# The order of the tensors in SBUF, in a decode attention kernel that streams K and V

## The chip, the cores and the metric

The kernel runs on one core of a Trainium2 chip. The metric is the device time of one execution in microseconds (us); before the change it is 2565.35 us, the median of three runs (2564.96 to 2565.8).

## The reference

Two independent attention blocks, A and B, for one new token each. Per block there are 8 batch rows, 32 heads of 128, and a cache of 4096 keys and values per head, all in bf16:

```python
q = (x @ wq).reshape(B, Sq, H, Dh).transpose(0, 2, 1, 3)
scores = einsum("bhqd,bhkd->bhqk", q, k_cache) * (Dh ** -0.5)
o = einsum("bhqk,bhkd->bhqd", softmax(scores, axis=-1), v_cache)
return o.transpose(0, 2, 1, 3).reshape(B, Sq, H * Dh) @ wo
```

The outputs of A and B stand side by side in a result of 8 x 1 x 2048. K and V of both blocks are 1.07 GB, each byte of which is read once; the weights `wq` and `wo` are 8.4 MB each.

## The kernel before

The work is cut into 64 turns (32 per block). A turn takes one batch row and eight heads: 8 x 4096 keys of 128 values are 8.39 MB, laid out as 128 partitions with 256 keys each, so each partition gets one contiguous row of 65,536 bytes. A load of K or V is one DMA of 128 such rows. `kbuf` holds two K loads (128 x 2 x 32768 bf16), `vbuf` one V load (128 x 32768 bf16); together they are 196,608 bytes of each partition. `wq` goes through `vbuf`, `wo` through the first half of `kbuf`, and the last V through `kbuf`.

In turn n, VectorE multiplies K in place with the query, which is the same in all rows of a head (line 337, four pieces of 64 keys). TensorE adds up 16 groups of 8 products with an identity matrix (line 347), VectorE adds the 8 that are left (line 359) and prepares the softmax (lines 364 to 368). ScalarE takes the exponentials of one head after the other (line 375). TensorE multiplies the probabilities of the turn before with V (`pv`, line 396), ScalarE copies the product (line 403), TensorE gathers the heads' diagonal blocks (line 411), VectorE scales them (line 423).

SP issues all big loads, in the order K of turn n, then V of turn n - 1 (lines 505 and 509, issued by line 223). The wait of V's load is for `pv` of the turn before, which has to be done with `vbuf`; the K load that follows in SP's order finds its half of `kbuf` already free. At the end `wo` of block B comes in five pieces (`pieces`, 16, 8, 4, 2 and 2 of 32 rows of 2048 bytes per partition) right behind the last V, and TensorE projects each piece as it lands (line 461).

Waits are worked out from the order of the operations (`Program.finish`) and the names of the tensors that they read and write; addresses play no part in them. The tensors get their addresses in the order in which the `sb` calls stand (lines 177 to 201): each begins where the one before it ends, rounded up to 32 bytes.

Of the kernel before, what the change touches and what calls it, by code (L numbers as in the profile page):

```python
# [8 lines left out]
BF16 = mybir.dt.bfloat16  # L9
FP32 = mybir.dt.float32  # L10
# [133 lines left out]
def _build(nc, caches, out):  # L144
    x0, k0, v0, wq0, wo0 = caches[0]
    B, Sq, D = x0.shape
    _, H, Sk, Dh = k0.shape
    NC = len(caches)
    HP = 8
    SEG = 128 // HP  # L150
    T = Sk // SEG
# [6 lines left out]
    TB = 512 // Dh  # L158
# [9 lines left out]
    with es:  # L168
        block = es.enter_context(nc.Block())

        def sb(name, shape, dt):
            return es.enter_context(nc.sbuf_tensor(name, shape, dt))
# [1 line left out]
        def ps(name, shape):  # L174
            return es.enter_context(nc.psum_tensor(name, shape, FP32))

        kbuf = sb("kbuf", [128, 2, T * Dh], BF16)
        vbuf = sb("vbuf", [128, T * Dh], BF16)
        prob = sb("prob", [128, T, HP], BF16)
        osb = sb("osb", [128, TB * Dh], FP32)  # L180
        asb = sb("asb", [128, CW], FP32)
        osum = sb("osum", [128, CW], FP32)
        orow = sb("orow", [128, CW], BF16)
        qT = sb("qT", [128, NC, H * B], BF16)
        qbc = sb("qbc", [128, 2, Dh], BF16)
        ident = sb("ident", [128, 128], BF16)
        ona = sb("ona", [128, NC * NG, HP, B], BF16)
        pick = sb("pick", [H, 128 + 3], BF16)
        turned = sb("turned", [H, B, Dh], BF16)
        onp = sb("onp", [128, RW, B], BF16)  # L190
        sel = sb("sel", [128, TB, HP], FP32)
        tmax = sb("tmax", [128, 32], FP32)
        rsum = sb("rsum", [128, 2, HP], FP32)
        rl = sb("rl", [128, 2, HP], FP32)
# [440 lines left out]
def bass_concat_heads__mha_block_cached__mha_block_cached__decode_kernel(  # L635
    nc, A_x, A_k_cache, A_v_cache, A_wq, A_wo, B_x, B_k_cache, B_v_cache, B_wq, B_wo, out,
):
    caches = [(A_x, A_k_cache, A_v_cache, A_wq, A_wo), (B_x, B_k_cache, B_v_cache, B_wq, B_wo)]
    _build(nc, caches, out)
# [28 lines left out]
```

## Time and profile before

| | |
|---|---|
| median of the runs | 2565.35 us |
| profiled execution, first to last instruction (span) | 2563.2 us |
| busy, TensorE matmuls / VectorE / ScalarE / GpSimd | 1470.8 / 1360.0 / 652.1 / 291.1 us |
| share of the 16 DMA engines, SP's queue | 99.9% |
| moved by DMA | 1107.52 MB in 19755 packets, 432 GB/s |

The page of the profile gives no time for the profiled execution beyond its span, so the 2.15 us between the span and the median of the runs stand for what lies around the first and the last instruction. Busy times are sums over the span; an engine that waits for a load shows the wait as idle time in front of its next instruction. A DMA packet here is one contiguous row of one partition (64 KB for K and V) or a write of a few bytes that reports completion. The packets of a stretch of the DMA view are those that start in it.

### The profile page before, as it was taken

What the parts mean: (1) busy time and instruction counts of PE and PEld (TensorE: products, weight loads), DVE (VectorE), ACT (ScalarE), POOL (GpSimd) and SP (SyncE); (2) the same over time, 40 slices, a digit from 0 to 9 for tenths busy, and PEclk for the clock granted to TensorE, in tenths of its full rate; (3) what the DMA queues carried; (4) which work ended last, traced back from release to release, by engine and by line L of the source; (5) the groups of instructions that cost most, each with busy time, mean ns of one, the idle gap of its engine ahead of it and who ended that gap; (6) DMA issues with size and microseconds to landing.
All of it is one profiled execution on the core that took longest, in us unless ns stands there. A gap on an engine that the chain in (4) does not pass through costs nothing.

```text
span 2563.2 us, 19013 instructions
## 1 busy us (share of the span) xinstructions
PE 1470.8 (57%) x9440; PEld 291.3 (11%) x5600; DVE 1360.0 (53%) x913; ACT 652.1 (25%) x1127; POOL 291.1 (11%) x112
## 2 busy tenths in 40 slices
PE   3565565565565565565565565555655655655656
PEld 0101101101101101101011011011011011011012
DVE  3456455455465465465464564564564564554551
ACT  0322322312312313313313313213223223223122
POOL 0111011011011011011011011011011010110110
PEclk8787787787787887887887887877877877878878
DMA  9999999999999999999999999999999999999999
GB/s 425 428 438 430 438 430 437 430 437 431 436 432 436 432 436 432 435 433 435 432 436 432 436 432 436 431 437 431 437 431 437 430 438 430 438 430 438 430 437 386
DMA packets 19755, 1107.52 MB, mean 432 GB/s; under 512 B 2256, under 2 KB 2320, under 8 KB 2592
## 3 DMA queue, kind: packets, MB, share of 16 engines
q1 hardware_dynamic: 19616, 1107.31, 99.9%
q8 instruction: 7, 0.11, 0.0%
q10 hardware_dynamic: 128, 0.06, 0.0%
q14 instruction: 4, 0.03, 0.0%
HBM read 1107.33 MB, written 0.03 MB: 432 GB/s over the span
## 4 chain that ended last, share of the span: by engine, by line
DMA 63%; PE 17%; DVE 14%; issue 6%; SPq 0%; another core or an unknown queue 0%; DVEq 0%
DMA kbuf<-in_B_k_cache_dram 31%; DMA kbuf<-in_A_k_cache_dram 30%; PE red L347 12%; DVE kbuf L337 12%; PE oacc L396 4%; DMA kbuf<-in_B_wo_dram 2%; DVE osb L359 2%; SPq L223 0%; DVE on L423 0%; PE acc L461 0%; DVEq L601 0%; PE oacc L275 0%; PE late L275 0%; PE bps L286 0%
## 5 line engine op out<-in xcount | busy, mean ns | idle before, releaser
L337 DVE TENSOR_TENSOR kbuf<-kbuf,qbc 128x8192 bf16<-128x8192 bf16 x256 | 1128.2, 4408 | 782.9 <-DMA kbuf<-in_A_k_cache_dram 389.8
L347 PE MATMUL red<-kbuf,ident 128*128 128x512 bf16 x4096 | 1050.9, 419 | 392.9 <-DVE kbuf L337 218.7
L375 ACT ACTIVATE prob<-osb,bias 128x256 bf16<-128x256 f32 x512 | 598.7, 1583 | 930.4 <-PE oacc L396 895.6
L425 POOL COPY ona<-on 128x8 bf16<-128x8 bf16 x64 | 278.7, 4354 | 2218.2 <-DVE on L423 2218.2
L411 PE MATMUL sps<-sel,osb 128*128 128x8 f32 x512 | 116.6, 357 | 649.9 <-ACT osb L403 649.7
L359 DVE TENSOR_REDUCE osb<-red 128x64 f32<-128x512 f32 x256 | 176.0, 687 | 305.9 <-PE red L347 305.9
L375 ACT ACTIVATION_READ_ACCUMULATOR prob<-osb,bias 128x1 f32 x512 | 252.9, 494 | 0.0
L329 ACT ACTIVATE qbc<-bps 128x256 bf16<-128x256 f32 x32 | 12.3, 383 | 897.6 <-PE bps L325 897.6
L396 PE MATMUL oacc<-vbuf,prob 128*32 128x512 bf16 x4032 | 231.8, 383 | 10.5 <-DMA vbuf<-in_B_v_cache_dram 10.5
L411 PEld LDWEIGHTS sps<-sel,osb 128*128 128x128 f32 x512 | 112.4, 323 | 669.7 <-issue 667.8
L347 PEld LDWEIGHTS red<-kbuf,ident 128*128 128x128 bf16 x256 | 25.1, 98 | 1191.0 <-issue 1170.3
L396 PEld LDWEIGHTS oacc<-vbuf,prob 128*32 128x32 bf16 x4032 | 102.5, 97 | 324.6 <-issue 219.1
L403 ACT ACTIVATE osb<-oacc 128x512 f32<-128x512 f32 x64 | 38.2, 597 | 15.3 <-PE oacc L396 8.2
L381 PE MATMUL sps<-rsum,ones 128*128 128x8 f32 x128 | 36.6, 360 | 5.4 <-ACT prob L375 5.4
L381 PEld LDWEIGHTS sps<-rsum,ones 128*128 128x128 f32 x128 | 34.7, 331 | 5.5 <-ACT prob L375 5.5
L364 DVE TENSOR_REDUCE rmax<-osb 128x1 f32<-128x256 f32 x64 | 26.9, 420 | 7.6
L423 DVE TENSOR_TENSOR on<-sps,rl 128x8 bf16<-128x8 f32 x64 | 10.1, 158 | 27.9 <-PE sps L381 27.9
L365 DVE STREAM_TRANSPOSE tmax<-rmax 128x32 f32<-128x32 f32 x64 | 13.5, 212 | 7.7
L366 DVE TENSOR_REDUCE nmax<-tmax 128x2 f32<-128x32 f32 x64 | 11.9, 186 | 7.6
L318 POOL COPY qg<-qT 128x256 bf16<-128x256 bf16 x32 | 12.5, 392 | 28.0 <-DVE qT L290 27.4
L368 DVE SCALAR_TENSOR_TENSOR bias<-nmax,neg 128x8 f32<-128x8 f32 x64 | 10.7, 168 | 7.7
L275 PE MATMUL oacc<-vbuf,orow 128*8 128x512 bf16 x64 | 7.7, 472 | 11.4 <-DMA vbuf<-in_A_wq_dram 11.4
(52 smaller groups left out, 104.1 us busy)
## 6 DMA issues: line engine op xcount, KB each, us to landing
kbuf<-in_B_wo_dram SPq DMA_DIRECT2D x1, 4096.0 KB, 39.5
kbuf<-in_B_wo_dram SPq DMA_DIRECT2D x1, 2048.0 KB, 44.0
kbuf<-in_B_wo_dram SPq DMA_DIRECT2D x1, 1024.0 KB, 46.1
kbuf<-in_B_wo_dram SPq DMA_DIRECT2D x2, 512.0 KB, 47.2
kbuf<-in_A_k_cache_dram SPq DMA_DIRECT2D x32, 49.1
vbuf<-in_A_v_cache_dram SPq DMA_DIRECT2D x32, 30.2
kbuf<-in_B_k_cache_dram SPq DMA_DIRECT2D x32, 49.1
vbuf<-in_B_v_cache_dram SPq DMA_DIRECT2D x31, 30.1
```

The lines of the kernel that those rows point to most:

```text
L318: P.add("pool", lambda e: e.tensor_copy(qg[:], src.unsqueeze(3).to_broadcast([128, 2, HP, SEG])), reads=[f"qT{c}"], writes=["qg"])
L337: P.add("dve", lambda e: e.tensor_tensor(kv, kv, qbc[:, n % 2, :].unsqueeze(1).to_broadcast([128, CT, Dh]), ALU.mult), reads=[f"k{n % 2}", ...
L347: first = e.matmul(rv, ident[:], pj[:, :, 0, :], start=True, stop=False).ins
L359: P.add("dve", lambda e: e.tensor_reduce(score[:, ch * CT:(ch + 1) * CT], rv, AX.X, ALU.add), writes=[f"score{ch}"], banks=[f"red{i}"])
L364: P.add("dve", lambda e: e.tensor_reduce(rmax[:], score, AX.X, ALU.max), reads=scores, writes=["rmax"])
L365: P.add("dve", lambda e: e.transpose(tmax[:], rmax[:].to_broadcast([128, 32])), reads=["rmax"], writes=["tmax"])
L375: P.add("act", lambda e, h=h: e.activation(prob[:, :, h], score, ACTF.Exp, bias=bias[:, h:h + 1], scale=scale, accum_out=rsum[:, i, h:h + 1]),
L381: P.add("pe", lambda e: e.matmul(sps[:, i * HP:(i + 1) * HP], ones[:].to_broadcast([128, 128]), rsum[:, i, :], start=True, stop=True), rea ...
L396: last = e.matmul(oacc[32 * q:32 * q + TB * HP, 0:TB * Dh], prob[:, t:t + TB, :].rearrange("p t h -> p (t h)"), buf[:, t * Dh:(t + TB) * D ...
L403: P.add("act", lambda e: e.activation(osb[:], oacc[:], ACTF.Copy), writes=scores, banks=["oacc"])
L411: last = e.matmul(sps[:, o:o + HP], osb[:, t * Dh:(t + 1) * Dh], sel[:, t, :], start=(t == 0), stop=(t == TB - 1))
L425: P.add("pool", lambda e: e.tensor_copy(ona[:, gi, :, b], on[:, i, :]), reads=[f"on{i}"], writes=[f"ona{gi}"])
```

## The change

Nine tensors that stood behind V (`prob`, `osb`, `asb`, `osum`, `orow`, `qT`, `turned`, `ident`, `sel`) are now allocated ahead of `kbuf` and `vbuf`. No size, type, instruction or wait is changed, and the instructions stand in the same order on every engine.

```diff
-        kbuf = sb("kbuf", [128, 2, T * Dh], BF16)
-        vbuf = sb("vbuf", [128, T * Dh], BF16)
         prob = sb("prob", [128, T, HP], BF16)
         osb = sb("osb", [128, TB * Dh], FP32)
         asb = sb("asb", [128, CW], FP32)
         osum = sb("osum", [128, CW], FP32)
         orow = sb("orow", [128, CW], BF16)
         qT = sb("qT", [128, NC, H * B], BF16)
+        turned = sb("turned", [H, B, Dh], BF16)
+        ident = sb("ident", [128, 128], BF16)
+        sel = sb("sel", [128, TB, HP], FP32)
+        kbuf = sb("kbuf", [128, 2, T * Dh], BF16)
+        vbuf = sb("vbuf", [128, T * Dh], BF16)
         qbc = sb("qbc", [128, 2, Dh], BF16)
-        ident = sb("ident", [128, 128], BF16)
         ona = sb("ona", [128, NC * NG, HP, B], BF16)
         pick = sb("pick", [H, 128 + 3], BF16)
-        turned = sb("turned", [H, B, Dh], BF16)
         onp = sb("onp", [128, RW, B], BF16)
-        sel = sb("sel", [128, TB, HP], FP32)
```

The addresses follow from the sizes. In each partition the first 16,384 bytes are reserved and four constants take 32 bytes each, so the first tensor begins at 16,512 = 4 x 4096 + 128. The nine tensors take 4096 + 2048 + 1024 + 1024 + 512 + 1024 + 2048 + 256 + 128 = 12,160 bytes, which with the 128 makes 3 x 4096.

| byte in the partition | before | after |
|---|---|---|
| `kbuf`, first half | 16,512 = 4 x 4096 + 128 | 28,672 = 7 x 4096 |
| `kbuf`, second half | 82,048 = 20 x 4096 + 128 | 94,208 = 23 x 4096 |
| `vbuf` | 147,584 = 36 x 4096 + 128 | 159,744 = 39 x 4096 |
| `prob` | 213,120 = 52 x 4096 + 128 | 16,512 = 4 x 4096 + 128 |
| `orow` | 221,312 | 24,704 |
| `ident` | 223,360 | 28,288 |

## The prediction

> **What bounds the kernel now.** I read the slices of the page first, then the DMA queues, the chain of waits, and last single stretches of the DMA queue. The page comes first:
>
> ```profile
> DMA  9999999999999999999999999999999999999999
> ...
> DMA packets 19755, 1107.52 MB, mean 432 GB/s; under 512 B 2256, under 2 KB 2320, under 8 KB 2592
> ...
> q1 hardware_dynamic: 19616, 1107.31, 99.9%
> ...
> q14 instruction: 4, 0.03, 0.0%
> ...
> L337 DVE TENSOR_TENSOR kbuf<-kbuf,qbc 128x8192 bf16<-128x8192 bf16 x256 | 1128.2, 4408 | 782.9 <-DMA kbuf<-in_A_k_cache_dram 389.8
> ```
>
> The reader is to see that all 16 DMA engines are busy in every slice, with one queue (SP's) at 99.9%, while the costliest VectorE line is idle for 782.9 us, mostly for K to land. The ends of the chain and one turn in the middle say whether the queue ever runs dry. The chain's columns are start, length, work:
>
> ```profile
> 1.21 42.38 DMA kbuf<-in_A_k_cache_dram
> ...
> 1011.25 1.02 DVE kbuf L337
> ...
> 1035.84 3.60 PE oacc L396 x64
> ...
> 1039.50 0.33 SPq L223
> ...
> 1039.87 48.69 DMA kbuf<-in_A_k_cache_dram
> ...
> 2512.09 47.52 DMA kbuf<-in_B_wo_dram
> ```
> ```profile
> 1049.95 4.43 DVE L337 TENSOR_TENSOR kbuf<-kbuf,qbc 128x8192 bf16<-128x8192 bf16 x1 [11.82 <-DMA kbuf<-in_A_k_cache_dram]
> ```
>
> K of one turn is there at 1011.25. The engines then work until PV (line 396) lets SP issue the next V (1039.50) and K (1039.87), 28.6 us later. At that moment the K before is still on its way: DVE gets it at 1049.95. So the queue holds 10.1 us of work whenever new work is added, and the turn of 38.70 us (1011.25 to 1049.95) is the time of two 8.39 MB loads, nothing else. Loads run from 1.21 to 2512.09 + 47.52 = 2559.61 us; only 3.6 us of the span come behind them. The time is bytes and packets through one queue, and the change can move it only through what a packet costs, or through an engine that loses more than 10.1 us a turn.
>
> **What a packet costs.** The view of the DMA queue over a stretch counts the packets that start in it, and gives their summed time as a share of 16 engines, so a stretch with packets of one size gives the time of one. Ten turns (64 KB packets, a partition's row of K or V), a stretch in the last pieces of `wo` (4 KB) and one with a single completion write (under 512 B):
>
> ```profile
> DMA packets 2880, 167.77 MB, mean 433 GB/s; under 512 B 320, under 2 KB 320, under 8 KB 320
> ...
> q1 hardware_dynamic: 2880, 167.77, 100.2%
> ```
> ```profile
> DMA packets 135, 0.46 MB, mean 229 GB/s; under 512 B 23, under 2 KB 23, under 8 KB 135
> ...
> q1 hardware_dynamic: 135, 0.46, 56.6%
> ```
> ```profile
> q1 hardware_dynamic: 1, 0.00, 9.4%
> ```
>
> The stretches are 387.07 us (from 1000), 2 us (from 2557) and 0.006 us (from 2547.32). The completion write takes 0.094 x 16 x 6 = 9.0 ns. The 64 KB packet: 1.002 x 16 x 387.07 = 6205.5 us, less 320 x 9 ns, over 2560 packets: 2422.9 ns. The 4 KB packet: 0.566 x 32 = 18.11 us, less 23 x 9 ns, over 112: 159.9 ns. Between them 61,440 bytes cost 2263.0 ns, that is 0.03683 ns a byte, and a part that does not grow with size remains: 159.9 - 4096 x 0.03683 = 9.0 ns a packet. Packets of one engine overlap a little in the records: 2560 in 387.07 us is one per 2419.2 ns on each engine, not 2422.9. Of these 65,536 x 0.03683 = 2413.9 ns are bytes and 9.0 / 8 = 1.1 ns is the completion write that comes once in eight packets, so 4.2 ns of fixed cost pace the queue. Whatever address does to a packet must be sought in these 4.2 to 9.0 ns.
>
> **The change part by part.** No instruction, transfer, wait or size changes, on any engine or queue; SP issues the same loads in the same order. What changes is addresses.
>
> 1. K's two halves and V move from 128 bytes past a multiple of 4096 (16,512, 82,048, 147,584) to multiples (28,672, 94,208, 159,744), as the build places them. Every packet of the 131 full loads (two `wq`, 64 K, 64 V, one `wo`) and of the five last `wo` pieces writes there: 131 x 128 = 16,768 packets and 640 smaller ones, 17,408 / 16 = 1088 on each engine, all in the stretch where the queue has no gap. One nanosecond per packet is 1.09 us of kernel time. No row shows a packet to a multiple of 4096, so the price is bounded: at most the whole fixed cost, 9.0 x 1088 = 9.8 us; at least nothing. Between them lies the loss of one half-filled stretch at the front of each row: 128 bytes at 0.03683 ns are 4.7 ns, or 5.1 us. I take this value. It is next to the 4.2 ns that pace the queue (4.6 us by that row), and the two ends would need the offset to explain all of a cost that also a 9.0 ns completion write has, or none of it.
>
> 2. Nine small tensors move ahead of K, and those that stay behind V shift with it. Engines that read them (the exponentials on ScalarE, the heads on VectorE, TensorE's `ident`) I cost at nothing: the 10.1 us of queued work per turn hide them. Without that cover each microsecond per turn would cost 63 us. `xs` in `prob` and `xT` in `orow` keep their offset of 128.
>
> 3. VectorE's multiply and TensorE's sums read K at the new address. Both end before the release at 1039.5, and an engine path of 28.6 us would have to grow by a third to be seen. Nothing.
>
> 4. The tail. Behind the last load stand 3.6 us of matmuls, a copy and two stores; they read the small tensors at their new place and touch the buffers only for the last 8 matmuls. Nothing.
>
> Sum: the span of 2563.2 loses 5.1 us and is 2558.1. The median of the runs, 2565.35, lies 2.15 us above the span; with the same 2.15 us the time is 2560.2.
>
> [...]
>
> **The rivals.**
>
> [...]
>
> *Nothing happens: the offset is not what costs.* A packet of another kind, that brings instructions and not K or V, is this single row, in 0.3 us from 639:
>
> ```profile
> DMA packets 1, 0.01 MB, mean 27 GB/s; under 512 B 0, under 2 KB 0, under 8 KB 0
> ...
> q14 instruction: 1, 0.01, 6.4%
> ```
>
> It takes 0.064 x 16 x 0.3 = 0.307 us for some 8 KB (the page has four such with 0.03 MB); the 8 KB packets of `wo` in the stretch of 0.65 us from 2553.6 are these:
>
> ```profile
> DMA packets 34, 0.23 MB, mean 353 GB/s; under 512 B 6, under 2 KB 6, under 8 KB 6
> ...
> q1 hardware_dynamic: 34, 0.23, 84.1%
> ```
>
> 0.841 x 16 x 0.65 = 8.75 us, less 6 x 9 ns, over 28: 310 ns. Other destination, same time: the fixed cost would be every packet's. It is not decided, since the trace does not show at which address the instruction packet lands. The time would be 2565.35.
>
> *Slower: the packets get longer.* Rows of K that DMA writes and rows that VectorE and TensorE read would begin at the same place of a 4096-byte block as before relative to each other (the halves lie 65,536 apart in both orders), but now the block's first bytes are also the rows'. Should this make writes wait, it costs 1.09 us for each nanosecond, and decides against the gain from 4.7 ns on; a second fixed cost of 9.0 ns per packet would give 2575.1. Against it speaks that meeting an engine costs nothing today: with DVE idle, in the 5 us from 2540,
>
> ```profile
> DMA packets 67, 2.20 MB, mean 439 GB/s; under 512 B 0, under 2 KB 0, under 8 KB 0
> ...
> q1 hardware_dynamic: 67, 2.20, 102.0%
> ```
>
> a 32 KB packet takes 1.02 x 80 / 67 = 1218 ns, and the line through the busy 64 KB packets gives 9.0 + 32,768 x 0.03683 = 1216 ns. [...]
>
> **How the numbers follow.** Half-filled stretch saved, 2560.2: 0.38. Whole fixed cost, 2555.6: 0.22. No effect, 2565.35: 0.27. Longer packets: 0.13. A fifth of a per cent, about what a measurement of this kernel can tell from no change, is 5.1 us, and my forecast lies on that border: I count half of its 0.38 as faster and half as the same. Faster is 0.22 + 0.19 = 0.41; the same is 0.19 + 0.27 and 0.01 of the longer packets, 0.47; slower is 0.12. The range goes from 2554.5 (whole fixed cost by the 9.4 ns, 10.2 us, and a little for the runs' scatter of 0.8 us) to 2567.0 (no effect and the same scatter twice); it leaves out the longer packets.
>
> **What would show it.** In the changed kernel the 64 KB packets should take 2418 ns instead of 2422.9, one per 2414.5 ns on each engine, a turn 38.63 us instead of 38.70, and the 4 KB packets 155 instead of 160 ns. The cost per byte must not move, only the fixed part. If the 4 KB packet stays at 160, the offset costs nothing; at 151 all of it went. The order of the chain, VectorE's 4408 ns and the 10.1 us of queued work should stay as they are; were the turn longer with unchanged packets, an engine would have become the bound. The prediction is wrong if the fixed cost belongs to the packet as such, or if the cost per byte depends on the address.

## The result and the profile after

The changed kernel takes 2560.47 us (median of 20 runs, 2560.29 to 2561.82) against 2564.86 us before in 20 runs (2564.55 to 2565.84). The ratio is 0.9983, its 95% interval 0.9976 to 0.999: 4.4 us less, or 0.17%. The page of the profile after, its span, its DMA rows and the costliest VectorE group:

```profile
span 2558.7 us, 19013 instructions
...
DMA packets 19755, 1107.52 MB, mean 433 GB/s; under 512 B 2256, under 2 KB 2320, under 8 KB 2592
...
q1 hardware_dynamic: 19616, 1107.31, 99.9%
...
L337 DVE TENSOR_TENSOR kbuf<-kbuf,qbc 128x8192 bf16<-128x8192 bf16 x256 | 1128.1, 4407 | 780.4 <-DMA kbuf<-in_B_k_cache_dram 379.7
```

Packets, bytes, the share of the queue and VectorE's work are what they were. The span is 4.5 us shorter. The chain of waits has the same shape, with the same work on it:

```profile
1.21 42.01 DMA kbuf<-in_A_k_cache_dram
...
1037.04 0.33 SPq L223
...
1037.41 49.32 DMA kbuf<-in_A_k_cache_dram
...
2506.63 48.49 DMA kbuf<-in_B_wo_dram
```

The last load lands at 2506.63 + 48.49 = 2555.12 us, before at 2559.61, so all of the gain lies in the loads and none in the 3.6 us behind them. It comes evenly: VectorE's first multiply of a turn, which starts when K lands, stands in the timeline of the kernel after like this, 14 turns apart,

```profile
1009.55 4.42 DVE L337 TENSOR_TENSOR kbuf<-kbuf,qbc 128x8192 bf16<-128x8192 bf16 x1 [12.01 <-DMA kbuf<-in_A_k_cache_dram]
...
1550.49 4.43 DVE L337 TENSOR_TENSOR kbuf<-kbuf,qbc 128x8192 bf16<-128x8192 bf16 x1 [12.81 <-DMA kbuf<-in_B_k_cache_dram]
```

and of the kernel before, 12 turns after the one at 1011.25:

```profile
1475.73 4.43 DVE L337 TENSOR_TENSOR kbuf<-kbuf,qbc 128x8192 bf16<-128x8192 bf16 x1 [13.07 <-DMA kbuf<-in_B_k_cache_dram]
```

A turn is 540.94 / 14 = 38.639 us after and 464.48 / 12 = 38.707 us before. A DMA engine moves 16 packets of 64 KB in it, so one packet comes every 2414.9 instead of every 2419.2 ns. The same stretch of the DMA queue as in the prediction (387.07 us from 1000), after:

```profile
DMA packets 2890, 168.43 MB, mean 435 GB/s; under 512 B 320, under 2 KB 320, under 8 KB 320
...
q1 hardware_dynamic: 2890, 168.43, 100.4%
```

1.004 x 16 x 387.07 = 6217.9 us, less 320 x 9 ns, over 2570 packets: 2418.3 ns a packet, from 2422.9.

### The profile page after: what moved, and what is told of

The parts are those of the page before. It is cut to its first block, busy times and chain, and to the rows that moved or that the text cites. A ratio compares the mean times of both kernels' runs of the same rounds, so it can differ in the third digit from the quotient of the medians.

```text
span 2558.7 us, 19013 instructions
## 1 busy us (share of the span) xinstructions
PE 1468.7 (57%) x9440; PEld 291.8 (11%) x5600; DVE 1359.9 (53%) x913; ACT 652.2 (25%) x1127; POOL 291.1 (11%) x112
## 4 chain that ended last, share of the span: by engine, by line
DMA 63%; PE 17%; DVE 14%; issue 6%; SPq 0%; another core or an unknown queue 0%; DVEq 0%
DMA kbuf<-in_B_k_cache_dram 31%; DMA kbuf<-in_A_k_cache_dram 30%; PE red L347 12%; DVE kbuf L337 12%; PE oacc L396 4%; DMA kbuf<-in_B_wo_dram 2%; DVE osb L359 2%; SPq L223 0%; DVE on L423 0%; PE acc L461 0%; DVEq L601 0%; PE oacc L275 0%; PE late L275 0%; SPq L586 0%
## 5 line engine op out<-in xcount | busy, mean ns | idle before, releaser
L423 DVE TENSOR_TENSOR on<-sps,rl 128x8 bf16<-128x8 f32 x64 | 10.1, 158 | 27.9 <-PE sps L381 27.9
```

## The experiments

Theory: a row of K or V that begins off a grid of addresses costs its packet some 4 ns, and the price is the DMA's own. Rivals: the small tensors' new place makes the gain; the grid is one of 4096 bytes; the price is in engines and DMA meeting in the buffers. Beside each run the kernel before ran on the same chip, at 2564.87 to 2564.9 us in the median.

**The order without the addresses.** The changed order, with 128 empty bytes ahead of K.

```diff
+        gap = sb("gap", [128, 64], BF16)
         kbuf = sb("kbuf", [128, 2, T * Dh], BF16)
```

> The order of the changed kernel, with 128 empty bytes ahead of K, so that K and V begin 128 bytes past a multiple of 4096 again. Theory of the offset (a row of K or V that begins off a grid costs each packet about 4 ns): back to the time before, 2564.9 us, 64 KB packets at 2422 to 2423 ns in the records. Rival, the place of the small tensors makes the gain: 2560.5 us, packets at 2419 ns.

Measured: 2564.9 us (11 runs, 2564.57 to 2565.58), ratio 1.0 (0.9991 to 1.0009). Its stretch of 387.07 us:

```profile
DMA packets 2880, 167.77 MB, mean 433 GB/s; under 512 B 320, under 2 KB 320, under 8 KB 320
...
q1 hardware_dynamic: 2880, 167.77, 100.2%
```

These are the rows of the kernel before, to the digit. The whole gain is gone with 128 bytes, so it is the address of K and V that counts and not the order of the tensors.

**The addresses without the order, at a coarser and a finer distance.** The kernel before, with 128, 96, 160 and 192 empty bytes ahead of K (the first of them is shown).

```diff
+        gap = sb("gap", [128, 64], BF16)
         kbuf = sb("kbuf", [128, 2, T * Dh], BF16)
         vbuf = sb("vbuf", [128, T * Dh], BF16)
         prob = sb("prob", [128, T, HP], BF16)
```

> The order of the kernel before, with 128 empty bytes ahead of K: K at 16640 and V at 147712, multiples of 256 but of no larger power of two. If the grid is one of 256 bytes or less: 2560.5 us as with the change. If 512, 1024 or 4096 matter: 2564.9 us as before.

> The order before, K and V 224 bytes past a multiple of 256. If the bytes between the grid and the row's start are what is paid (224 instead of 128): 2560.5 + 4.4 x 224 / 128 = 2568.2 us. If a row off the grid costs one extra piece whatever the distance: 2564.9 us.

> The order before, K and V 32 bytes past a multiple of 256. Bytes ahead of the start: 2560.5 + 4.4 x 32 / 128 = 2561.6 us. One extra piece: 2564.9 us.

> The order before, K and V 64 bytes past a multiple of 256. So far 128 past costs 4.3 us over the grid, and 32 and 224 past cost 5.5 us. If a first cost is for leaving the 256-byte grid and a second one for leaving a grid of 64 bytes: 2564.9 us, as at 128. If the second is for leaving a grid of 128 bytes: 2566.1 us, as at 32 and 224. If distance counted: 2562.7 us.

| K and V past a multiple of 256 | other | us, median (range) | ratio (95% interval) |
|---|---|---|---|
| 0 | multiple of 4096 (the change) | 2560.47 (2560.29 to 2561.82) | 0.9983 (0.9976 to 0.999) |
| 0 | 256 past a multiple of 4096 | 2560.7 (2560.25 to 2561.89) | 0.9984 (0.9975 to 0.9993) |
| 64 | | 2565.05 (2564.88 to 2565.92) | 1.0001 (0.9992 to 1.001) |
| 128 | the kernel before | 2564.86 (2564.55 to 2565.84) | 1 |
| 32 | | 2566.09 (2565.98 to 2567.46) | 1.0005 (0.9996 to 1.0014) |
| 224 | | 2566.06 (2565.87 to 2567.0) | 1.0005 (0.9996 to 1.0014) |

Multiples of 256 are enough; 4096 gives nothing beyond. The number of bytes between the grid and the row's start does not count: 32 and 224 bytes cost the same, and 64 the same as 128, so the theory that bytes ahead of the start are paid has failed (2561.6 and 2568.2 us were to be expected). What is paid is, on average, one price per packet for being off the grid. Single packets differ: in the kernel before, the three that start in the 0.5 us from 1003 have a share of 90.7% and so 0.907 x 16 x 500 / 3 = 2418.7 ns each, as on the grid (2418.3); the three in the 0.6 us from 1000.5 have 75.8%, which makes 2425.6 ns. A second, smaller price shows at 32 and 224: 1.2 us in both medians. Each interval of the ratio still holds no difference, but the spans of these 22 runs, 2564.0 to 2564.5 us, all lie above those of the 33 runs of the kernel before beside them, 2562.7 to 2563.6. The two offsets are no multiples of 64, and they are also the two that lie nearest to a multiple of 256 (32 bytes on either side); no run tells which of the two it is.

**Engines out of the way.** Both orders, with most of the engines' access to K and V left out: VectorE multiplies 4 of 64 keys, TensorE adds 2 of 16 groups and does 4 of 64 PV matmuls. What they compute is not attention.

```diff
-            kv = chunk(n, ch).rearrange("p (t d) -> p t d", d=Dh)
+            kv = chunk(n, ch).rearrange("p (t d) -> p t d", d=Dh)[:, 0:4, :]
...
-                for j in range(1, NJ):
+                for j in range(NJ - 1, NJ):
...
-                for j in range(CT):
+                for j in range(4):
```

The two other lines that change fit a shape and the matmuls' start and stop flags to this.

> The kernel before with nearly all of the engines' access to K and V left out: VectorE multiplies 4 of each 64 keys, TensorE adds 2 of the 16 groups of products, and PV takes 4 of its 64 matmuls, so the result is not attention; loads, waits and their order stay. If the offset's price is the DMA's own: 2564.9 us, 4.4 us above the same kernel with the changed order. If it comes from engines and DMA meeting in the buffers: 2560.5 us, as the changed order.

> The changed kernel with the same work left out. DMA's own price: 4.4 us below the light kernel of the old order, about 2560.5 us less what the shorter tail saves. Engines and DMA meeting: no difference between the two light kernels.

Measured: 2564.68 us (10 runs, 2564.55 to 2565.09) in the old order and 2560.4 us (10 runs, 2560.22 to 2560.73) in the new one, 4.3 us apart. The page of the old order without the work has the same full queue, and VectorE busy for 13% of the span instead of 53%, TensorE's matmuls for 19% instead of 57%:

```profile
PE 480.1 (19%) x2016; PEld 202.4 (8%) x1760; DVE 341.5 (13%) x913; ACT 652.1 (25%) x1127; POOL 39.2 (2%) x112
...
DMA  9999999999999999999999999999999999999999
```

So the price does not come from VectorE or TensorE meeting the DMA in the buffers; it is the DMA's own. VectorE went from 1360.0 to 341.5 us of work, and the times stayed within 0.2 us of the full kernels': the engines are off the path in both orders.

**Eight times the packets.** Each full load but `wo` of block A, which stays whole, as eight DMAs of 8 KB rows, in both orders: 130 loads.

```diff
-            return P.add(eng, lambda e: e.dma_start(dst, src), reads=reads, writes=writes, dma=sem)
...
+            w = T * Dh // 8
+            op = P.add(eng, lambda e: [e.dma_start(dst[:, i * w:(i + 1) * w], src[:, i * w:(i + 1) * w]) for i in range(8)],
+                       reads=reads, writes=writes, dma=sem)
```

> The kernel before with each full load issued as eight DMAs of 8 KB rows, so that there are eight times as many packets at the same bytes. A packet's fixed cost outside the overlap of the records was 4 to 9 ns; seven more packets on each of 1048: 31 to 66 us slower than before, 2596 to 2631 us.

> The changed kernel with the same cut into 8 KB rows. If the offset is paid per packet, the distance to the uncut pair's 4.4 us grows eightfold: 35 us below the kernel before with 8 KB rows. If it is paid per byte, per load or by engines: 4.4 us below it.

Measured: 2638.31 us (4 runs, 2638.15 to 2638.44; ratio 1.0286, 1.027 to 1.0302) and 2603.3 us (4 runs, 2603.22 to 2603.46; ratio 1.0149, 1.0134 to 1.0165). They are 35.0 us apart, eight times the 4.4 of the uncut pair, as an average price per packet has it. The first estimate, 2596 to 2631 us for the old order, was too low: it left out the completion writes, which also come eight times as often, 910 more on each engine at 9.0 ns or 8.2 us. From the pairs the fixed cost of a packet follows without any line through the records: 7 x 8 x 130 = 7280 packets more on each engine cost 73.45 us off the grid and 42.83 us on it, 10.1 and 5.9 ns each. With the 1.1 ns of completion writes taken off, 9.0 ns and 4.8 ns. The offset makes up 4.2 of the 9.0. (The cut also changes the order in which K and V are read from memory; both kernels of the pair share that, so it can sit in the 4.8 but not in the 4.2.)

**One buffer off the grid.** The changed kernel, once with V 128 bytes off and once with K.

```diff
         kbuf = sb("kbuf", [128, 2, T * Dh], BF16)
+        gap = sb("gap", [128, 64], BF16)
         vbuf = sb("vbuf", [128, T * Dh], BF16)
```
```diff
+        gap = sb("gap", [128, 64], BF16)
         kbuf = sb("kbuf", [128, 2, T * Dh], BF16)
+        gap2 = sb("gap2", [128, 64], BF16)
         vbuf = sb("vbuf", [128, T * Dh], BF16)
```

> The changed kernel with 128 empty bytes between K and V: K's 65 full loads and the pieces of wo stay on the grid, the 66 loads that use the V buffer leave it (wq twice, V 63 times) or the like. A price per packet: half of the 4.4 us comes back, 2562.7 us. If the two buffers matter only together, for one with respect to the other: 2560.5 or 2564.9 us.

> The mirror of the run with V off the grid: the changed kernel's order with K 128 bytes past a multiple of 256 and V at a multiple of 256. V off the grid alone cost 0.6 of the 4.4 us. If K's loads carry the rest, because they go to another buffer or because TensorE and VectorE read and write there: 2564.3 us. If it takes both buffers off the grid (the cost is not a sum over packets): 2561.1 us, as with V alone.

Measured: 2561.1 us with V off (11 runs, 2560.96 to 2562.77; ratio 0.9986, 0.9977 to 0.9995), 2561.43 us with K off (11 runs, 2561.15 to 2561.77; ratio 0.9986, 0.9977 to 0.9995). Half of the packets are off the grid in either (65 of the 131 full loads go to V's buffer, 66 and the pieces to K's), and neither pays half: 0.6 and 1.0 us, where both together cost 4.4. The price per packet does not simply add up; of the cases tried, only the one with all packets off the grid pays it in full.

**One buffer off the grid, long loads.** V off by 128 bytes and 8 KB rows, so that an engine writes 64 packets off the grid, then 64 on it, instead of 8 and 8.

> V alone 128 bytes off the grid, with 8 KB rows. With 64 KB rows V alone cost 0.6 us and K alone 1.0 us, both together 4.4 us. If the lateness of the off-grid packets is made good while on-grid packets follow (eight packets of each kind in turn on an engine, some 30 ns of lateness), 64 packets in a row with some 250 ns of it may be too much to make good: up to half of the 35 us, 2620.8 us. If a fixed share of the price is all that one buffer off the grid pays: 0.6 / 4.4 of 35 us, 2608 us.

Measured: 2610.5 us (4 runs, 2610.34 to 2611.07; ratio 1.0177, 1.016 to 1.0194), 7.2 us over the same kernel with both on the grid: more than the fixed share would give, and less than half of 35. The trace shows where it is paid. A load is 1024 such packets; VectorE's multiply starts at 988.80 when a K load is there,

```profile
988.80 4.43 DVE L345 TENSOR_TENSOR kbuf<-kbuf,qbc 128x8192 bf16<-128x8192 bf16 x1 [12.95 <-DMA kbuf<-in_A_k_cache_dram]
```

and by the count of packets V's load runs from 986.7 to 1006.3, the next K from there to 1026. The DMA queue in the first half of this V load (9.8 us), in its last quarter (4.9 us), and in the first half of the K load (9.8 us):

```profile
DMA packets 576, 4.19 MB, mean 428 GB/s; under 512 B 64, under 2 KB 64, under 8 KB 64
...
q1 hardware_dynamic: 576, 4.19, 101.3%
...
DMA packets 285, 2.07 MB, mean 423 GB/s; under 512 B 32, under 2 KB 32, under 8 KB 32
...
q1 hardware_dynamic: 285, 2.07, 101.6%
...
DMA packets 575, 4.19 MB, mean 427 GB/s; under 512 B 64, under 2 KB 64, under 8 KB 64
...
q1 hardware_dynamic: 575, 4.19, 101.1%
```

A packet takes 1.013 x 16 x 9.8 = 158.84 us, less 64 x 9 ns, over 512: 309.1 ns in the first half of V. In the last quarter it takes 313.7 ns, in K again 309.1. The kernels with 8 KB rows and both buffers off or both on the grid, over 196 us from 1000, give the two levels:

```profile
DMA packets 11355, 82.69 MB, mean 422 GB/s; under 512 B 1262, under 2 KB 1262, under 8 KB 1262
...
q1 hardware_dynamic: 11354, 82.68, 101.3%
```
```profile
DMA packets 11504, 83.78 MB, mean 427 GB/s; under 512 B 1278, under 2 KB 1278, under 8 KB 1278
...
q1 hardware_dynamic: 11503, 83.77, 101.1%
```

1.013 x 16 x 196 = 3176.8 us less 1262 x 9 ns, over 10,092: 313.7 ns off the grid; 309.0 ns on it by the same way. With both on the grid, a packet also takes 309.1 ns in each of the three short stretches, and in steps of 2.45 us through two turns from 986.7 it takes 308.8 to 309.1 in all but one (311.2). So it is not the place in the turn that makes the end of V's load slow. Off-grid packets run at the on-grid pace for the first half of the load at least, and at the off-grid pace at its end. The run's time says the same: 7.2 us over 65 loads are 111 ns a load, the price of 26 of its 64 packets.

The kernel with V off the grid and 64 KB rows has the same shape. There VectorE's multiply starts at 1009.85, so by the same count V's load runs from 1007.7 to 1027. The DMA queue in 11 us from 1008 and in 5 us from 1022:

```profile
DMA packets 78, 4.65 MB, mean 423 GB/s; under 512 B 7, under 2 KB 7, under 8 KB 7
...
q1 hardware_dynamic: 78, 4.65, 97.6%
```
```profile
DMA packets 43, 2.36 MB, mean 472 GB/s; under 512 B 7, under 2 KB 7, under 8 KB 7
...
q1 hardware_dynamic: 43, 2.36, 109.1%
```

A packet takes 0.976 x 176 = 171.78 us, less 7 x 9 ns, over 71: 2418.5 ns at first, and 2422.7 at the end. So the beginning of an off-grid load to V behind an on-grid one to K is free in both kernels. A reserve that takes up a fixed amount of lateness does not explain it: of the whole price of a load, 64 x 4.2 = 269 ns with the short rows and 8 x 4.0 = 32 ns with the long ones, 158 and 23 ns are not paid (0.6 us over 65 loads is 9 ns a load). What makes the beginning free is not shown.

## Why the prediction was right or wrong

- *What bounds the kernel: right.* One queue without a gap from 1.21 us to the last pieces of `wo`, where it runs dry for the last 2 us or so (a share of 56.6% in the prediction's own row), and engines whose work can be taken away without effect.
- *The time: right within 0.3 us* of the 2560.47 measured, and near the border between faster and the same that it named. 4.4 us came instead of 5.1, which is 4.0 ns a packet over 1088 packets instead of 4.7. The times agree better than the gains by luck: the 2565.35 us that the prediction started from lay 0.5 us above the median of 20 runs.
- *The reason for the 4.7 ns: wrong.* The step that failed is the one that took "one half-filled stretch at the front of each row: 128 bytes". No run shows such a stretch; it was the author's assumption. Bytes ahead of the start are not what is paid: at 32 and 224 bytes the price is not a quarter and seven quarters, and at 64 it is that of 128 (2566.09, 2566.06, 2565.05 and 2564.86 us). In its place stands a price per packet for leaving the grid of 256 bytes, on average 4.2 ns by the cut kernels, and that this is near 128 bytes' time is chance. With another offset before, the same reasoning would have missed.
- *The bounds: right, the row between them mis-sized.* The line through the records gave a fixed cost of 9.0 ns; the cut kernels give 9.0 too. But the 4.2 ns said to "pace the queue" were too low. The fault is the row of 4 KB packets: in its stretch the queue was already running dry (56.6%), and an off-grid packet there takes 159.9 ns. In the 0.4 us from 2556.4, with the queue still full,

```profile
DMA packets 42, 0.16 MB, mean 399 GB/s; under 512 B 3, under 2 KB 3, under 8 KB 42
...
q1 hardware_dynamic: 42, 0.16, 99.7%
```

  it takes 0.997 x 6.4 = 6.381 us, less 3 x 9 ns, over 39: 162.9 ns. With this row a byte costs 0.036784 ns, and 2419.2 - 2410.7 - 1.1 = 7.4 ns pace the queue, not far from the 9.0 by run times. All 9.0 ns pace the queue off the grid, and 4.8 of them stay on it. The bytes of a 64 KB packet then take 2409.1 ns before (2419.2 - 9.0 - 1.1) and 2409.0 after (2414.9 - 4.8 - 1.1): the cost per byte did not move, as forecast. That the mixed line also gave 9.0, and that the same 4.2 came out as the price, are chance too.
- *The whole fixed cost goes: wrong,* 4.2 of the 9.0 ns went and 4.8 stay on the grid. No run shows the 9.4 ns behind the lower end of the range. *Nothing happens: wrong,* though half of it holds: a cost of 4.8 ns stays, and the instruction packet's 307 ns for some 8 KB are near the 309.0 of a packet of 8 KB on the grid. Its 310 ns of the 8 KB `wo` packets came from a stretch at 84.1%; with the queue full of them, such a packet takes 313.7 ns off the grid.
- *Slower, packets longer: wrong.* On average a 64 KB packet takes 2418.3 ns after and took 2422.9 before. Nor does meeting the engines cost the DMA anything that shows: the two kernels without most of the engine work, 2564.68 and 2560.4 us, take the times of the full ones, 2564.87 and 2560.47.
- *Small tensors, VectorE's and TensorE's access, the tail at nothing: right.* The order alone changes nothing, and VectorE's 4408 ns are 4407.
- *What would show it.* 64 KB packets of 2418 ns and a turn of 38.63 us were seen, 2418.3 and 38.639; one per 2414.5 ns on each engine, 2414.9. The 4 KB packets were to go from 160 to 155 ns. In the 0.8 us from 2552 of the kernel after, with the queue full,

```profile
DMA packets 89, 0.33 MB, mean 415 GB/s; under 512 B 8, under 2 KB 8, under 8 KB 89
...
q1 hardware_dynamic: 89, 0.33, 101.2%
```

  they take 1.012 x 12.8 = 12.95 us, less 8 x 9 ns, over 81: 159.0 ns, against 162.9 before in a full stretch: 3.9 ns less, the price. Against the 159.9 of the prediction's row they hardly moved, which by its own test would have meant that the offset costs nothing. That test was a bad one, since its row was taken where the queue ran dry.

## What to carry to other kernels

Where one DMA queue is full from end to end, let SBUF tensors that loads write begin at a multiple of 256 bytes: 128 empty bytes ahead of them did the same here (2560.7 us) as an order worked out for 4096 (2560.47). With all loads moved to the grid the gain here was 4.0 ns a packet with rows of 64 KB, a sixth of a per cent, and 4.2 ns with rows of 8 KB, 35 us of 2638; long rows come first. To price a packet, cut the rows and compare run times; where records must do, take them only from stretches in which the queue is full.

## What the runs showed of the hardware that was not expected

Being off the grid by 32, 64, 128 or 224 bytes costs 4.4 to 5.6 us over the kernel on the grid, and the price does not grow with the bytes between grid and start. It is an average: off the grid the means of three 64 KB packets are 2418.7 and 2425.6 ns in the two short stretches read here. Where V's loads alone were off the grid, they paid nothing in the first half or more of a load, with rows of 64 KB and of 8 KB, so a price measured with all packets off the grid must not be split among buffers. And where the queue ran dry at the end, off-grid packets of 4 KB went from 162.9 ns back to 159.9. Whether the price arises in each DMA engine or in something that the 16 share, and what sets the on-grid pace, stays open.
